# Broadcasting softmax factors through DRAM in an LSH attention kernel with a convolutional gate

## The chip, the cores and the metric

The kernel runs on one core of a Trainium2 chip. The metric is the time of one execution on the device in microseconds; the times given are medians of several runs. One further execution was profiled, and all rows of a profile come from that one.

## The reference

Attention with a hash mask runs over 4 batches, 8 heads, 768 positions and a head size of 64; a query sees only the keys whose 6 sign bits of a projection agree with its own. A gated feed-forward net (512 to 1024 to 512) follows, with a convolution of three taps along the sequence in the gate.

```python
mask = q_bucket[:, :, :, None] == k_bucket[:, :, None, :]
scores = scale * np.matmul(q, k.transpose(0, 1, 3, 2))
scores = np.where(mask, scores, -1000000000.0)
scores = scores - np.max(scores, axis=-1, keepdims=True)
attn = np.exp(scores)
attn = attn / (np.sum(attn, axis=-1, keepdims=True) + 1e-09)
x = np.matmul(attn, v)          # heads side by side: B, S, 512
h = np.maximum(x @ w_in, 0.0)
conv_out = sum(conv_w[k] * hp[:, k:k + S, :] for k in range(3))   # hp: h padded by one row
out = (h * (1.0 / (1.0 + np.exp(-conv_out)))) @ w_out
```

The weights of the feed-forward net come as 64-bit floats. The kernel splits them, as it splits x, q and k, into a high and a low part, so that matmuls on the fast 32-bit format keep their precision.

## The kernel before

**Pairs, groups, units.** Two heads form a *pair*; there are 16 (4 batches of 4). A *unit* is a tile of 128 queries of one head against all 768 keys, so a pair has 12 units. Four units (two heads, two query tiles, 256 queries) form a *group*, three groups to a pair. All units stand in one list, and one loop over `i` emits the instructions in a fixed order by hand; each engine executes its own instructions in that order. Iteration `i` emits, in this order: the score matmuls of unit `i` (`products`, L257), its maximum on VectorE (L270 and L274), the reciprocals of a group that has ended two units before (`reciprocals`, L291 and L292), the transposes of unit `i-3` (L297) and their copy to SBUF on ScalarE (L304), and the exponential of unit `i` on ScalarE (L277), which also sums the rows into one column of `sums`.

**The burst.** Once in four iterations, `AVS` gives a number of steps other than zero. Then the matmuls of probabilities and values of the group that was complete an iteration earlier go out in one burst: `values` gives its steps. The first step, `spread` (L319), multiplies a broadcast column of `inv` (a 128x64 weight whose 64 columns are all the reciprocals of one query tile and head) with the identity, four times. This puts the reciprocal of each query, repeated over the 64 rows of a head, into the second half of the PSUM tile `av`. Six `chunk` steps (L325) fill the first half. `factors` (L330, ScalarE, emitted at the start of the next iteration) copies the second half to the SBUF tile `rs`; `out` (L333, VectorE, in the next burst) multiplies the first half by it, and `parts` (L336 and L337, GpSimd) splits the result into the high and low part of x.

**Late pairs.** Pairs from number 7 on (`LATE`) normalise the probabilities themselves on GpSimd (L285) ahead of the transposes and use none of `reciprocals`, `spread`, `factors` and `rs`. The code that the change touches therefore runs for 7 pairs, 21 groups, in the first 230 us.

**What else is emitted around the burst.** In each burst some steps of decoding the feed-forward weights go out (`background`): integer operations on VectorE (L91 to L101), then a cast on ScalarE (L110) and two operations on GpSimd (L111 and L112). A weight block is loaded by a DMA on ScalarE's queue (`fetch`, L132). Beside them the next pair is prepared. The transposed q and k of a pair lie in `R`, which has one buffer. `split` forms the high part of a head on GpSimd (`hi`, L171), sends copies of it to the operand tiles by DMAs on SP's queue (L174), then forms the low part in `R` itself (L176) and sends that (L178). `hash` multiplies `R` with the projection (L186, TensorE, three iterations into the pair before the one that it is for). The seventh iteration of a pair ends the second `split`, and SP is then given the load of values (L165) and the next load of `R` (L158), which has to wait until the copies out of `R` have landed.

**The ending of a batch.** When all pairs of a batch and three pairs more are done, the feed-forward net of that batch runs (`ffn`; L368, L398 are its matmuls). The last group before it is handed to the net as `fill`, which emits that group's `values` steps at once within the net's first step. Of the pairs that use the reciprocals, this concerns one group.

Of the kernel before, what the change touches and what calls it, by code (L numbers as in the profile page):

```python
# [7 lines left out]
F32 = mybir.dt.float32  # L8
# [6 lines left out]
B, H, S, D = 4, 8, 768, 64  # L15
NB = 6
DM, DFF = 512, 1024
P = 128
NP = H // 2
NCK = S // P  # L20
HS = S // 2
QB = 256
# [7 lines left out]
LAG, EB = 3, 5  # L30
DEFER = 3
FLAG = 3
LATE = NP + DEFER
AVS = (1 + NCK, 0, 0, 0)
PREP = 1
PREP_N = 6
W0 = 7
# [5 lines left out]
def lsh_attention_conv_ffn(ctx, tc, qk, v, hw, w_in, conv_w, w_out, consts, ident_in, out):  # L43
    nc = tc.nc
    PSUM = bass.MemoryType.PSUM
    cp = ctx.enter_context(tc.tile_pool(name="const", bufs=1))
    wp = ctx.enter_context(tc.tile_pool(name="work", bufs=1))
    ps = ctx.enter_context(tc.tile_pool(name="ps", bufs=2, space=PSUM))

    turns = {}  # L50

    def ring(pool, bufs, shape, dtype, tag, name):

        k = turns[tag] = (turns.get(tag, -1) + 1) % bufs
        return pool.tile(shape, dtype, tag=f"{tag}{k}", name=name, bufs=1)
# [88 lines left out]
    class Pair:  # L144
        def __init__(self, b, p):
            self.b, self.p, self.nm = b, p, f"{b}_{p}"
            self.late = b * NP + p >= LATE
            self.inv = None

        def load(self):  # L150
            nm = self.nm
# [93 lines left out]
    class Unit:  # L245
# [14 lines left out]
        def maximum(self, prev):  # L260

            self.st = ring(wp, 8, [P, 4], F32, "st", f"st{self.nm}")
            pr = self.pair
            if self.tq == 0 and self.h == 0 and not pr.late:
                pr.sums = sums4[self.qb % 3]
            self.sums = None if pr.late else pr.sums
            self.sum = self.st[:, 2:3] if pr.late else pr.sums[:, 2 * self.tq + self.h, 0:1]
            e = wp.tile([P, 776], F32, tag="e", name=f"e{self.nm}", bufs=EB)
            self.e = e[:, :S]
            nc.vector.tensor_scalar(self.e.rearrange("p (a b) -> p a b", a=2), self.sp[:, :, :HS],  # L270
                                    MASKED, None, ALU.max, ALU.max, accum_out=self.st[:, 0:1])
            if prev and prev.pair.late:
                prev.total()
            nc.vector.tensor_scalar(self.st[:, 1:2], self.st[:, 0:1], -SCALE, None, ALU.mult)  # L274
# [12 lines left out]
        def reciprocals(self):  # L287
# [3 lines left out]
            nc.vector.tensor_reduce(pr.inv, self.sums, mybir.AxisListType.X, ALU.add)  # L291
            nc.vector.reciprocal(pr.inv, pr.inv)  # L292

        def transposes(self):
            self.tp = ring(ps, 3, [P, 2, 512], F32, "S", f"t{self.nm}")
            for c in range(NCK):
                nc.tensor.transpose(self.tp[:, c // 3, c % 3 * P:(c % 3 + 1) * P],  # L297
                                    self.e[:, c * P:(c + 1) * P], ident)
# [5 lines left out]
            nc.scalar.copy(pr.at[self.h][:, :, :, self.tq * P:(self.tq + 1) * P],  # L304
                           self.tp[:, :, :3 * P].rearrange("p j (c q) -> p j c q", c=3))

    def values(pr, qb, ats, inv):

        if qb == 0:
            pr.x = [ring(wp, NP + DEFER, [P, S], F32R, f"x{k}", f"x{k}{pr.nm}")  # L310
# [1 line left out]
        vt, (xh, xl) = pr.v, pr.x  # L312
        av = ring(ps, 2, [P, 512], F32, "M", f"v{pr.nm}_{qb}")

        def spread():

            for t in range(QB // P):
                for h in range(2):
                    nc.tensor.matmul(av[h * D:(h + 1) * D, QB + t * P:QB + (t + 1) * P],  # L319
                                     inv[:, 2 * t + h:2 * t + h + 1].to_broadcast([P, D]), ident,  # L320
                                     start=True, stop=True, tile_position=(0, h * D))

        def chunk(c):
            for h in range(2):
                nc.tensor.matmul(av[h * D:(h + 1) * D, :QB], vt[:, c, h, :],  # L325
                                 ats[h][:, c // 3, c % 3, :],
                                 start=(c == 0), stop=(c == NCK - 1), tile_position=(0, h * D))

        def factors():
            nc.scalar.copy(rs, av[:, QB:2 * QB])  # L330

        def out():
            nc.vector.tensor_tensor(rs, av[:, :QB], rs, ALU.mult)  # L333
# [12 lines left out]
        chunks = [lambda c=c: chunk(c) for c in range(NCK)]  # L346
        if pr.late:
            return chunks, (out_high, out_low, lambda: None)
        rs = ring(wp, 2, [P, QB], F32, "rs", f"rs{pr.nm}_{qb}")
        return [spread, *chunks], (factors, out, parts)  # L350


    g2, prep = [None], [iter(()), iter(())]
# [93 lines left out]
    first = pairs[0].prepare_now()  # L447
    next(first)
    pairs[1].load()
    av, outs, lows, early = [], [], [], None  # L450
    n = len(units)
    ffn_after = {min((b + 1) * NP - 1 + DEFER, B * NP - 1): b for b in range(B)}
    for i in range(n + LAG):
# [20 lines left out]
            prev.total()  # L474
        two = units[i - 2] if 2 <= i <= n + 1 else None
        if two and not two.pair.late and two.tq == QB // P - 1 and two.h == 1:
            two.reciprocals()
        if w and w is not early:
            w.transposes()
            w.to_sbuf()  # L480
# [1 line left out]
            u.exponential()  # L482
        if prev and prev.pair.late:
            prev.normalise()
        if i in (0, 2):
            next(first, None)
        parts = []
# [7 lines left out]
        prepare(0)  # L495
        if ending:
            prepare(0)
        for _ in range(1 + NCK if ending else AVS[(i - LAG) % 4]):
            if av:
                steps, last = av[0]  # L500
                steps.pop(0)()
                if not steps:
                    outs.append(last)
                    av.pop(0)
# [13 lines left out]
        fetch(i % 2 if i < 8 else burst)  # L518
        if w and w.tq == QB // P - 1 and w.h == 1:
            if not ending:  # L520
                av.append(values(w.pair, w.qb, w.pair.at, w.pair.inv))
            else:
                def fill():
                    steps, last = values(w.pair, w.qb, w.pair.at, w.pair.inv)
                    for step in [*steps, *last]:
                        step()

                bi = ffn_after[wi]
                early = units[i + 1 - LAG] if i + 1 - LAG < n else None

                def transposes_ahead():
                    if early:
                        early.transposes()
                        early.to_sbuf()
                        turns["S"] -= 1

                ffn(bi, [pairs[bi * NP + c].x for c in range(NCC)], fill, transposes_ahead)
# [43 lines left out]
```

## Time and profile before

| what | us |
|---|---|
| median of 3 runs (740.05 to 745.73) | 740.08 |
| the profiled execution | 739.48 |
| its span | 737.5 |
| TensorE matmul busy | 710.9 |
| VectorE busy | 487.3 |
| ScalarE busy | 498.5 |
| GpSimd busy | 331.9 |

In the profile's lines PE is TensorE's matmuls and PEld its weight loads, DVE is VectorE, ACT ScalarE, POOL GpSimd, SP the engine that only issues DMAs. A name with a q (SPq, ACTq) is the engine's queue, where the issue of a DMA counts. `L297` is line 297 of the kernel before. `t<-ident,e` reads: tile t is written from tiles ident and e; numbers in tile names are left out. What stands in brackets or behind a bar as "idle before" is the time for which the engine stood still ahead of the instruction, and what released it. TensorE's granted clock is 0.997 over the span. The chain of waits goes back from the last instruction, at each step to what released it. A matmul on 32-bit floats appears as two records, so four `spread` matmuls give eight.

### The profile page before, as it was taken

To read this page: it belongs to the slowest core of one execution; us is meant where nothing else is said; L and a number is where in the kernel's file an instruction comes from. 1 tells how busy PE (TensorE), PEld (TensorE's weight loads), DVE (VectorE), ACT (ScalarE), POOL (GpSimd) and SP (SyncE) were. 2 spreads that over 40 slices of the span, in tenths; PEclk is the share of its full clock that TensorE was granted. 3 is DMA by queue.
4 is the path that set the end of the run, shared out by engine and by line. 5 is a ranking of instruction groups with operands and counts; after the bars stand their busy time and mean duration, and the time that the engine had idled before them with its cause. 6 is when DMAs were issued, how large, how long until landed. Compare 5 with 4: busy or idle time off the path is not lost.

```text
span 737.5 us, 13543 instructions
## 1 busy us (share of the span) xinstructions
PE 710.9 (96%) x4720; PEld 589.0 (80%) x4720; DVE 487.3 (66%) x1211; ACT 498.5 (68%) x937; POOL 331.9 (45%) x334
## 2 busy tenths in 40 slices
PE   6998999899899999999999999999999999999997
PEld 3787777678778988777877998778778899878996
DVE  7977878788775755666665666466666566555663
ACT  5788578678684554877877554778778655585554
POOL 4265456357463522475673532355755232241321
PEclk9999999999999999999999999999999999999999
DMA  4867666663552310237545130324463001100011
GB/s 143 222 187 202 165 186 166 165 166 89 147 146 52 86 44 36 72 77 189 139 105 149 34 94 3 108 60 113 117 180 95 1 0 44 44 1 1 0 44 43
DMA packets 30355, 72.17 MB, mean 98 GB/s; under 512 B 5936, under 2 KB 7504, under 8 KB 30288
## 3 DMA queue, kind: packets, MB, share of 16 engines
q1 hardware_dynamic: 27696, 62.88, 32.0%
q10 hardware_dynamic: 2592, 8.44, 3.3%
q8 instruction: 37, 0.61, 0.3%
q14 instruction: 30, 0.25, 0.1%
HBM read 27.40 MB, written 6.29 MB: 46 GB/s over the span
## 4 chain that ended last, share of the span: by engine, by line
PE 69%; DMA 11%; POOL 7%; issue 5%; DVE 4%; SPq 3%; ACT 1%; POOLq 0%; DVEq 0%; ACTq 0%
PE h L368 19%; PE o L398 18%; PE v L325 11%; PE s L257 10%; PE t L297 9%; DMA R<-in_qk 6%; DMA k<-R 4%; POOL R L176 2%; SPq L174 2%; DVE e L270 1%; DMA K<-hi 1%; PE hash L186 1%; POOL hi L171 1%; ACT e L277 1%; SPq L178 1%
## 5 line engine op out<-in xcount | busy, mean ns | idle before, releaser
L270 DVE TENSOR_SCALAR_CACHE_REDUCE e<-s 128x768 f32<-128x768 f32 x192 | 183.2, 954 | 81.2 <-PE s L257 70.6
L277 ACT ACTIVATE e<-e,st 128x768 f32<-128x768 f32 x192 | 181.3, 944 | 10.3 <-DVE st L284 5.0
L304 ACT COPY at<-t 128x768 f32<-128x768 f32 x192 | 152.3, 794 | 47.0 <-PE t L297 47.0
L297 PE MATMUL t<-ident,e 128*128 128x128 f32 x1152 | 160.0, 275 | 3.6 <-POOL e L285 1.5
L377 DVE SCALAR_TENSOR_TENSOR ht<-ht,cw 128x384 f32<-128x384 f32 (+1 forms) x128 | 114.7, 896 | 71.2 <-ACT ht L375 69.0
L387 POOL TENSOR_TENSOR g<-ht,g 128x384 fp32r<-128x384 f32 x64 | 71.5, 1117 | 179.5 <-ACT g L386 141.8
L297 PEld LDWEIGHTS t<-ident,e 128*128 128x128 f32 x1152 | 130.6, 141 | 22.3 <-POOL e L285 7.4
L285 POOL TENSOR_SCALAR e<-e,st 128x768 f32<-128x768 f32 x108 | 98.3, 911 | 103.1 <-DVE st L284 51.4
L398 PE MATMUL o<-wo,g 128*128 128x512 f32 x576 | 142.4, 394 | 0.0
L368 PE MATMUL h<-xh,wi 128*128 128x386 f32 x512 | 141.9, 340 | 0.0
L325 PE MATMUL v<-at,v 128*64 128x256 f32 x1152 | 135.6, 385 | 0.0
L398 PEld LDWEIGHTS o<-wo,g 128*128 128x128 f32 x576 | 107.4, 188 | 20.3
L257 PE MATMUL s<-K,Q 128*128 128x384 f32 x384 | 116.7, 385 | 1.9 <-ACT e L277 1.0
L325 PEld LDWEIGHTS v<-at,v 128*64 128x64 f32 x1152 | 81.2, 138 | 42.4 <-issue 8.6
L257 PE MATMUL s<-k,q 96*128 96x384 f32 x384 | 100.2, 342 | 2.1 <-ACT q L237 1.9
L368 PEld LDWEIGHTS h<-xh,wi 128*128 128x128 f32 x512 | 94.1, 188 | 4.8 <-issue 1.8
L380 ACT ACTIVATE ht<-ht 128x384 f32<-128x384 f32 x64 | 33.6, 526 | 91.4 <-DVE ht L377 91.4
L368 PE MATMUL h<-xl,wi 128*128 128x386 f32 x256 | 86.7, 339 | 0.0
L257 PEld LDWEIGHTS s<-K,Q 128*128 128x128 f32 x384 | 59.0, 192 | 23.2 <-issue 16.6
L257 PEld LDWEIGHTS s<-k,q 96*128 96x128 f32 x384 | 70.7, 191 | 3.5 <-ACT q L237 3.0
L381 DVE TENSOR_TENSOR ht<-ht 128x384 f32<-128x384 f32 x64 | 40.2, 629 | 33.4 <-ACT ht L380 33.4
L176 POOL TENSOR_TENSOR R<-R,hi 128x768 fp32r<-128x768 f32 x30 | 56.6, 1886 | 0.2
(75 smaller groups left out, 586.0 us busy)
## 6 DMA issues: line engine op xcount, KB each, us to landing
R<-in_qk SPq DMA_DIRECT2D x15, 768.0 KB
K<-hi SPq DMA_DIRECT2D x60, 192.0 KB
v<-in_v SPq DMA_DIRECT2D x16, 384.0 KB
out<-osb SPq DMA_DIRECT2D x24, 256.0 KB
Q<-hi SPq DMA_DIRECT2D x30, 192.0 KB
q<-hi SPq DMA_DIRECT2D x30, 192.0 KB
Q<-R SPq DMA_DIRECT2D x30, 192.0 KB
k<-R SPq DMA_DIRECT2D x30, 192.0 KB
```

The source lines that it names most:

```text
L176: nc.gpsimd.tensor_tensor(lo, R, hi.bitcast(F32), ALU.subtract)
L257: nc.tensor.matmul(self.sp[:, half, :HS], A[:, h, qs], C[:, h, half * HS:(half + 1) * HS], start=(kk == 0), stop=(kk == 1))
L270: nc.vector.tensor_scalar(self.e.rearrange("p (a b) -> p a b", a=2), self.sp[:, :, :HS], MASKED, None, ALU.max, ALU.max, accum_out=self.st ...
L277: nc.scalar.activation(self.e, self.e, AF.Exp, bias=self.st[:, 1:2], scale=SCALE, accum_out=self.sum)
L285: nc.gpsimd.tensor_scalar(self.e, self.e, self.st[:, 3:4], 0.0, ALU.mult, ALU.add)
L297: nc.tensor.transpose(self.tp[:, c // 3, c % 3 * P:(c % 3 + 1) * P], self.e[:, c * P:(c + 1) * P], ident)
L304: nc.scalar.copy(pr.at[self.h][:, :, :, self.tq * P:(self.tq + 1) * P], self.tp[:, :, :3 * P].rearrange("p j (c q) -> p j c q", c=3))
L325: nc.tensor.matmul(av[h * D:(h + 1) * D, :QB], vt[:, c, h, :], ats[h][:, c // 3, c % 3, :], start=(c == 0), stop=(c == NCK - 1), tile_posi ...
L368: nc.tensor.matmul(hp[:, :HW], w, x[:, c0:c0 + HW], start=(n == 0), stop=(n == 3 * NCC - 1))
L377: nc.vector.scalar_tensor_tensor(t[:, a:z], ht[:, o + k - 1 + a:o + k - 1 + z], cw[:, f, k:k + 1], t[:, a:z], ALU.mult, ALU.add)
L387: nc.gpsimd.tensor_tensor(g[:, 1, :], t, g[:, 0, :].bitcast(F32), ALU.subtract)
L398: nc.tensor.matmul(op, l, r, start=(f == 0 and n == 0), stop=(f == NFC - 1 and n == 2))
```

## The change

The reciprocals no longer go through TensorE. When a group's reciprocals are done, `reciprocals` now makes three things: a tile `row` of 2 x 2 x 128 floats in DRAM (a ring of four), a tile `rs` of 128 x 256 in SBUF (a ring of two, as before), and a list of steps. `write` sends `inv`, 128 partitions of four floats, to `row` in the order head, query tile, query. `read` issues two DMAs, one for each head: 256 floats of `row` are read into each of 64 partitions of `rs`. All three DMAs stand on ScalarE's queue. The main loop keeps these lists in `spreads` and executes one step of each per iteration, right after the exponential: `write` in the iteration of `reciprocals` itself, nothing in the next, `read` in the one after that. That is the iteration of the burst.

`spread` and `factors` go, `values` takes `rs` instead of `inv`, and a burst has six steps instead of seven. The columns of `sums` are ordered by head first, so that `inv` has the order of `row`. At the end of a batch the steps that are left are executed ahead of the feed-forward net, for the one group that `fill` takes over.

```diff
-AVS = (1 + NCK, 0, 0, 0)
+AVS = (NCK, 0, 0, 0)
+    dp = ctx.enter_context(tc.tile_pool(name="dram", bufs=1, space=bass.MemoryType.DRAM))
-            self.sum = self.st[:, 2:3] if pr.late else pr.sums[:, 2 * self.tq + self.h, 0:1]
+            self.sum = self.st[:, 2:3] if pr.late else pr.sums[:, 2 * self.h + self.tq, 0:1]
             nc.vector.reciprocal(pr.inv, pr.inv)
+            inv = pr.inv
+            row = ring(dp, 4, [2, QB // P, P], F32, "row", f"row{self.nm}")
+            rs = pr.rs = ring(wp, 2, [P, QB], F32, "rs", f"rs{self.nm}")
+
+            def write():
+                nc.scalar.dma_start(row.rearrange("h t q -> q (h t)"), inv)
+
+            def read():
+                for h in range(2):
+                    nc.scalar.dma_start(rs[h * D:(h + 1) * D],
+                                        row[h].rearrange("t q -> (t q)").unsqueeze(0).to_broadcast([D, QB]))
+
+            return [write, None, read]
-        def spread():
-
-            for t in range(QB // P):
-                for h in range(2):
-                    nc.tensor.matmul(av[h * D:(h + 1) * D, QB + t * P:QB + (t + 1) * P],
-                                     inv[:, 2 * t + h:2 * t + h + 1].to_broadcast([P, D]), ident,
-                                     start=True, stop=True, tile_position=(0, h * D))
-        def factors():
-            nc.scalar.copy(rs, av[:, QB:2 * QB])
-        rs = ring(wp, 2, [P, QB], F32, "rs", f"rs{pr.nm}_{qb}")
-        return [spread, *chunks], (factors, out, parts)
+        return chunks, (lambda: None, out, parts)
-            two.reciprocals()
+            spreads.append(two.reciprocals())
             u.exponential()
         if prev and prev.pair.late:
             prev.normalise()
+        for steps in spreads:
+            if steps:
+                step = steps.pop(0)
+                if step:
+                    step()
-        for _ in range(1 + NCK if ending else AVS[(i - LAG) % 4]):
+        for _ in range(NCK if ending else AVS[(i - LAG) % 4]):
-                av.append(values(w.pair, w.qb, w.pair.at, w.pair.inv))
+                av.append(values(w.pair, w.qb, w.pair.at, w.pair.rs))
             else:
+                for steps in spreads:
+                    while steps:
+                        step = steps.pop(0)
+                        if step:
+                            step()
```

More of the change, by code (lines that the diff above doesn't have):

```diff
@@ L147, in __init__ @@
             self.late = b * NP + p >= LATE
-            self.inv = None
+            self.inv = self.rs = None
         def load(self):
@@ L305, in to_sbuf, with values @@
                            self.tp[:, :, :3 * P].rearrange("p j (c q) -> p j c q", c=3))
-    def values(pr, qb, ats, inv):
+    def values(pr, qb, ats, rs):
         if qb == 0:
@@ L449, in lsh_attention_conv_ffn @@
     pairs[1].load()
-    av, outs, lows, early = [], [], [], None
+    av, outs, lows, early, spreads = [], [], [], None, []
     n = len(units)
@@ L520, in lsh_attention_conv_ffn @@
             if not ending:
-                av.append(values(w.pair, w.qb, w.pair.at, w.pair.inv))
+                av.append(values(w.pair, w.qb, w.pair.at, w.pair.rs))
             else:
+                for steps in spreads:
[3 more added lines that the diff above has]
+                            step()
                 def fill():
-                    steps, last = values(w.pair, w.qb, w.pair.at, w.pair.inv)
+                    steps, last = values(w.pair, w.qb, w.pair.at, w.pair.rs)
                     for step in [*steps, *last]:
```

## The prediction

> **What bounds the kernel now.** I read the page first, then the costs of the two operations that go, then the weight-load row of one burst, the waits of TensorE, and last the chain of waits through the first 230 us, where the changed code runs.
>
> ```profile
> span 737.5 us, 13543 instructions
> PE 710.9 (96%) x4720; PEld 589.0 (80%) x4720; DVE 487.3 (66%) x1211; ACT 498.5 (68%) x937; POOL 331.9 (45%) x334
> PE 69%; DMA 11%; POOL 7%; issue 5%; DVE 4%; SPq 3%; ACT 1%; POOLq 0%; DVEq 0%; ACTq 0%
> ```
>
> TensorE looks full, so removing matmuls looks like pure gain. But 18% of the chain that ended last is DMA and POOL, and that share has a place. The groups of instructions by line and form give what is removed; columns are count, then busy us and mean ns, then the idle time before them.
>
> ```profile
> L319 PE MATMUL v<-ident,inv 128*64 128x128 f32 x168 | 13.8, 285 | 0.0
> L330 ACT COPY rs<-v 128x256 f32<-128x256 f32 x21 | 7.8, 371 | 18.2 <-PE v L325 15.6 <-PE t L297 1.3 <-DMA rawi<-in_w_in 1.2
> ```
>
> The 168 records are 21 groups of 8. What one group holds TensorE for is read better from the weight loads of one burst in the timeline (start, duration, operation):
>
> ```profile
> 62.39 0.42 PEld L319 LDWEIGHTS v<-ident,inv 128*64 128x64 f32 x8 [0.17 <-issue]
> 62.77 2.41 PEld L325 LDWEIGHTS v<-at,v 128*64 128x64 f32 x24
> 65.57 0.30 PEld L257 LDWEIGHTS s<-K,Q 128*128 128x128 f32 x2 [0.38 <-issue]
> ```
>
> From the first broadcast weight to the first weight of the values, 62.77 - 62.39 = 0.38 us. The 0.17 us ahead of it I leave where it is, since the change of tile shape stays and the values come next. So 21 x 0.38 = 8.0 us of TensorE go at most, less than the 13.8 us of the busy column, whose ends overlap.
>
> Does TensorE have to wait for something else in that stage? The hash matmuls of the next pair of heads, one burst of eight per pair, answer that (timeline, idle time in brackets; then the same wait summed over 13 to 230 us as us, times, longest):
>
> ```profile
> 73.51 0.85 PE L186 MATMUL hash<-R,hw_sb 128*32 128x384 f32 x8 [2.18 <-DMA R<-in_qk]
> 103.10 0.85 PE L186 MATMUL hash<-R,hw_sb 128*32 128x384 f32 x8 [0.49 <-DMA R<-in_qk]
> 133.70 0.85 PE L186 MATMUL hash<-R,hw_sb 128*32 128x384 f32 x8 [1.82 <-DMA R<-in_qk]
> 161.97 0.85 PE L186 MATMUL hash<-R,hw_sb 128*32 128x384 f32 x8 [0.28 <-DMA R<-in_qk]
> 192.02 0.85 PE L186 MATMUL hash<-R,hw_sb 128*32 128x384 f32 x8 [1.87 <-DMA R<-in_qk]
> 220.17 0.85 PE L186 MATMUL hash<-R,hw_sb 128*32 128x384 f32 x8 [1.48 <-DMA R<-in_qk]
> PE hash L186 <- DMA R<-in_qk: 8.3, 7, 2.2
> ```
>
> From 73 us on, TensorE runs out of work at every pair because the load of R is late. The chain shows why; first its way into this state, then one full loop, then the end of it.
>
> ```profile
> 34.50 0.59 PE v L319 x8
> ...
> 44.20 0.59 PE v L319 x8
> ...
> 53.06 0.59 PE v L319 x8
> ...
> 62.73 0.60 SPq L178
> ...
> 63.38 3.98 DMA k<-R
> ...
> 67.37 6.00 DMA R<-in_qk
> ```
>
> ```profile
> 162.82 0.59 PE v L319 x8
> ...
> 173.68 2.89 issue
> ...
> 176.61 1.30 POOL upo L111
> ...
> 180.46 1.78 POOL R L176
> ...
> 183.54 3.93 DMA k<-R
> ...
> 187.53 4.36 DMA R<-in_qk
> ```
>
> ```profile
> 223.33 0.59 PE v L319 x8
> ```
>
> R has one buffer. It can be loaded again only when GpSimd has formed the low part in place (L176) and the copies of it (k<-R) have landed. GpSimd gets to L176 late because L111 ahead of it waits for ScalarE's cast of a weight block (L110), which belongs to the second burst of a pair. So a loop runs: R landed, hash, first burst of the pair, one group of four units, second burst, cast, L111, L176, copies, load of R. Only the first burst's matmuls are in it; the other two bursts of a pair run beside the copies and the load.
>
> **The change part by part.** Removed from TensorE: 0.38 us in each of 21 bursts. On the chain lie the bursts at 34.50, 44.20 and 53.06, one in each of the five loops between the six hash rows, and the one in the FFN's first step at 223.33: 9 x 0.38 = 3.4 us gained. The first burst (before 34.50) and two per loop, 12 x 0.38 = 4.6 us, only lengthen the wait for R.
>
> Removed from ScalarE: the copy `factors`, 0.37 us per group. Its row has 15.6 us of idle time before it that ended with TensorE, so ScalarE was waiting there anyway: nothing gained. The sums' new index and the six-step bursts cost nothing: no instruction is added by them, and no engine's order changes but for the eight records that go. The second half of the PSUM tile falls free, but the tile keeps its size and ring: nothing.
>
> Added, 21 times: one write of `inv` to DRAM and two reads of `row` into `rs`, all three on ScalarE's queue. ScalarE's order around a second burst, and the DMA rows to price it:
>
> ```profile
> 51.27 0.95 ACT L277 ACTIVATE e<-e,st 128x768 f32<-128x768 f32 x1
> ...
> 52.88 0.95 ACT L277 ACTIVATE e<-e,st 128x768 f32<-128x768 f32 x1
> ...
> 54.49 0.96 ACT L277 ACTIVATE e<-e,st 128x768 f32<-128x768 f32 x1
> ...
> 56.21 0.62 ACT L110 CAST wi<-upi 128x512 fp32r<-128x512 f32 x1 [0.68 <-DVE lowi L101]
> 57.67 0.33 ACTq L132 DMA_DIRECT2D rawi<-in_w_in  x1
> ```
>
> ```profile
> 61.40 1.23 SPq L174 DMA_DIRECT2D K<-hi  x2
> ```
>
> ```profile
> 136.47 1.95 DMA K<-hi
> ```
>
> ```profile
> q10 hardware_dynamic: 2592, 8.44, 3.3%
> ```
>
> ```profile
> 211.90:215.90 4.00, 4.00 (x35) 3.00 (x30) 2.97 (x5) 2.61 (x6) 1.53 (x2) 1.00 1.02 261
> 215.90:220.10 4.20, 2.68 (x19) 2.09 (x17) 3.25 (x15) 3.99 (x8) 3.53 (x5) 1.00 0.63 205
> ```
>
> The write follows the exponential two units after a group's last, here the one at 51.27; the wait it brings is for the reciprocals, which VectorE forms right behind the maximum that this exponential needs too, so they are done while it runs. Its issue (0.33 us for a load from this queue, 0.61 us for a 64-partition copy) hides behind the 0.95 us as well. Without that cover it would cost 0.3 to 0.6 us of ScalarE.
>
> The reads follow two exponentials later, at 54.49, and wait for the write to land. 54.49 - 51.27 = 3.2 us are there; a copy between SBUF tiles landed 1.95 us after its issue, so I take no hold here. No row shows a write of single floats to DRAM, so this is bounded below. Queued behind the two reads on ScalarE are the cast L110, the weight loads of L132 and the next unit's copy of transposes; GpSimd waits for the cast, and so does the loop. Two issues at 0.61 us end 1.2 us after the exponential starts, 0.3 us past its end (1.2 - 0.95). In the quoted burst the cast had 0.68 us of idle time ahead of it, in others none: between 0 and 1.2 us, I take 0.3 us per loop.
>
> The landed factors are wanted by VectorE's product (L333) a burst later, 62.39 - 53.06 = 9.3 us after. Behind it in its queue stand the decoding steps of a weight block, the next maximum and so the cast; cover of about 7 us after a landing like the 1.95 us one makes this wait nothing.
>
> What the transfers do to others: the last burst of a pair puts its reads beside the critical k<-R, when the 16 engines are full (1.02 in the first window; the column before the last is the DMA share). Two halves of 64 rows of 1 KB are 131 KB: at 261 GB/s 0.5 us if they are only added, 0 if they fit into gaps; I take 0.4 us. The write of the following group falls into the load of R. `inv` has four floats per partition that go to places 512 bytes apart, so I count 512 packets, 32 per engine. Queue q10 took 3.3% of 16 engines' 737.5 us for 2592 packets, 0.15 us each, mostly of 4 KB. That gives 32 x 0.15 = 4.8 us per engine if a packet of one float costs as much, and nearly 0 if the cost goes by bytes. With a share of 0.63 in the second window, 0.37 x 4.2 = 1.6 us per engine are free; I take 0.3 us of delay, near the lower end, because those gaps cover the first 1.6 us. Per loop 0.3 + 0.4 + 0.3 = 1.0 us, over the six loads of R 6.0 us. That the transfers themselves bring a gain is excluded: none of the old ones goes away.
>
> At the last group of the stage the read is flushed one unit after the write, not two, so ScalarE may hold there for most of a landing, under 2 us; TensorE itself waits for R until 220.17 at that place, so I put it at nothing. SP's and POOL's queues issue nothing new and nothing is moved past them, other than through what they wait for.
>
> Sum on the profiled execution, 739.48 us (span 737.5, 2.0 outside it; 0.6 below the median of 740.08): 739.5 - 3.4 + 6.0 = 742.1 us.
>
> **The rivals.** *All matmuls pay.* If the loop of R were not the limit, all 8.0 us would go: 731.5 us. For it: two of the six waits are only 0.28 and 0.49 us. Against: they alternate with waits of 1.8 us and more, and each shorter group of TensorE makes R later relative to it. If the loop limits but the transfers are free, 739.5 - 3.4 = 736.1; I count this into the forecast's own range.
>
> *The write lands late and holds ScalarE: slower.* The read sits in front of the cast at the second burst of each pair. With 512 packets at 0.15 us, landing takes 1.95 + 4.8 = 6.75 us, 3.55 us more than the 3.2 available, six times: 21 us, 763 us. It decides against the kernel by 1% from a hold of 0.9 us per loop, (747.5 - 742.1) / 6, a landing of 4.1 us or 67 ns per packet. For it: nothing in the trace writes single floats, so nothing shows that they are cheap. Against: the packets carry 2 KB in all. The Trainium skill, DMA: Bandwidth & Descriptors, section Rules for kernel authors, states that an access with a strided last dimension becomes one descriptor per element and advises against it; no run here shows it yet, and by that rule this rival's packet count holds.
>
> *The change doesn't do what it says*: if something still kept the two-step order waiting, such as the product L333 arriving before the factors, TensorE would idle at bursts. 9.3 us of cover speak against; I give it no chance of its own.
>
> **How the numbers follow.** About 1%, 7.4 us, is what can be told from no change. Forecast 0.58, from 736 to 747. All matmuls pay 0.12, 731 to 735: a little over half of it, 0.07, is faster by over 1%. Late landing 0.30, 747.5 to 763, nearly all slower. So faster 0.07, same 0.63, slower 0.30. For 8 in 10 the range takes the forecast's own, the upper half of the first rival and half of the late landing: 734 to 754. The forecast's own range is 736 to 747.
>
> **What would show it.** Right: no records of L319's kind; weight loads of the values 0.38 us earlier in a burst; hash waits for R longer than before, near 2 us in every pair; k<-R or the load of R a few tenths longer; the last hash (220.17) about 3 us later at most. Wrong: hash waits that vanish (then all 8 us pay), or the cast L110 held on ScalarE by a write in DRAM, seen as idle time ended by a DMA ahead of it, and L111 later in step. If the period from hash to hash, about 29.3 us ((220.17 - 73.51) / 5), shrinks to three bare groups of TensorE, the loop was not the limit.

## The result and the profile after

The kernel after takes 837.85 us (median of 4 runs, 830.33 to 841.61), the kernel before beside it 740.07 us: ratio 1.129, 95% interval 1.124 to 1.134. I had predicted 742.1 us and a range up to 754. Both the side and the size are wrong: 98 us are lost where 2 were expected.

The page of the kernel after, with the granted clock by slices and the row of ScalarE's DMA queue (packets, MB, share of 16 engines):

```profile
span 839.8 us, 13315 instructions
PE 739.0 (88%) x4552; PEld 609.0 (73%) x4552; DVE 488.4 (58%) x1211; ACT 493.6 (59%) x916; POOL 330.5 (39%) x334
PEclk8898899779888888999999999999999999999999
q10 hardware_dynamic: 17040, 11.24, 5.9%
```

What was to go is gone: 4720 - 4552 = 168 matmuls, 937 - 916 = 21 copies. The other engines are as busy as before and the span is 102 us longer, so the time is waiting. The clock shows where: it is at 0.7 to 0.9 in the first sixteen slices, some 336 us with the stage of the changed code, and then does not fall below 0.9. Queue q10 has 17040 - 2592 = 14448 packets more, 688 for each of 21 groups: 512 for the write as counted, 128 for the rows that are read, and 48 more, 16 for each of the three transfers (the kernel with the write alone, further down, has 528 for each group).

The hash matmuls of TensorE in the timeline, the marks of the loop of R (L187 here is L186 of before):

```profile
98.92 1.03 PE L187 MATMUL hash<-R,hw_sb 128*32 128x384 f32 x8
...
231.83 1.51 PE L187 MATMUL hash<-R,hw_sb 128*32 128x384 f32 x8 [6.08 <-DMA R<-in_qk]
274.26 1.51 PE L187 MATMUL hash<-R,hw_sb 128*32 128x384 f32 x8 [5.50 <-DMA R<-in_qk]
317.46 0.99 PE L187 MATMUL hash<-R,hw_sb 128*32 128x384 f32 x8
```

The last of them comes at 317.46 instead of 220.17 us. So 97.3 of the 102 us are lost in this stage, and a pair takes (317.46 - 98.92) / 5 = 43.7 us instead of 29.3.

ScalarE and its queue in the timeline: the issue of a write (L300), of the two reads that wait for it (L304), and the cast behind them (L111 here, L110 before).

```profile
62.22 0.38 ACTq L300 DMA_DIRECT2D row<-inv  x1
...
74.20 1.10 ACTq L304 DMA_DIRECT2D rs<-row  x2
75.39 0.62 ACT L111 CAST wi<-upi 128x512 fp32r<-128x512 f32 x1 [6.93 <-DMA q<-bits]
...
241.21 0.37 ACTq L300 DMA_DIRECT2D row<-inv  x1
...
251.85 1.36 ACTq L304 DMA_DIRECT2D rs<-row  x2
```

Between issue and reads lie 12.0 and 10.6 us, in the 21 groups 7.8 to 12.9. I had 3.2 us there and a landing of 1.95. The cast stands behind the reads, as one rival had it; its bracket names a transfer of the bits (`q<-bits`), the last to land of those that were waited for there. The other transfers suffer too; rows of the chain of waits (start, duration):

```profile
82.22 9.01 DMA k<-R
91.28 6.46 DMA R<-in_qk
...
220.32 11.38 DMA R<-in_qk
...
264.62 9.51 DMA R<-in_qk
```

In the prediction's rows the same two took 3.93 to 3.98 and 4.36 to 6.00 us. And yet the DMA engines are idle most of that time. The window between a write's issue and its reads (columns: us, busy of PE, PEld, DVE, ACT, POOL, granted clock, DMA share, GB/s):

```profile
241.20:251.90 10.70, 7.54 (x58) 6.51 (x56) 7.68 (x20) 4.30 (x9) 2.79 (x3) 1.00 0.24 47
```

A share of 0.24 means that something else than the time of packets on the engines holds the write up. The write issued at 108.69 us shows it by itself. This row is ScalarE's queue between 109.5 and 110.1 us, with the packets of that write; between 110.1 and 117.0 us the queue has none, and yet the reads start only at 117.13.

```profile
q10 hardware_dynamic: 528, 0.00, 45.8%
```

The waits over the whole kernel (us, times, longest) show who pays in the end:

```profile
DVE e L271 <- PE s L258: 151.7, 81, 6.7
POOL upi L112 <- ACT wi L111: 82.3, 8, 19.7
PEld s L258 <- ACT at L319: 59.5, 21, 6.2
```

ScalarE's copies stand behind the held reads, the scores' weights wait for them (59.5 us), and VectorE waits for the scores. SP's queue waits as well: four of its waits, 11.1 us in all, end with the landing of a write, though nothing on SP reads `row`. The prediction has no such path, and why SP waits there no run tests. The same view for SP's queue (13 to 330 us):

```profile
SPq L179 <- DMA row<-inv: 5.9, 2, 4.1
SPq L196 <- DMA row<-inv: 5.2, 2, 3.7
```

### The profile page after: what moved, and what is told of

Same layout as the page of the kernel before. It is cut to its first block, busy times and chain, and to the rows that moved or that the text cites. A ratio compares the mean times of both kernels' runs of the same rounds, so it can differ in the third digit from the quotient of the medians.

```text
span 839.8 us, 13315 instructions
## 1 busy us (share of the span) xinstructions
PE 739.0 (88%) x4552; PEld 609.0 (73%) x4552; DVE 488.4 (58%) x1211; ACT 493.6 (59%) x916; POOL 330.5 (39%) x334
## 3 DMA queue, kind: packets, MB, share of 16 engines
q10 hardware_dynamic: 17040, 11.24, 5.9%
## 4 chain that ended last, share of the span: by engine, by line
PE 57%; DMA 18%; issue 10%; POOL 7%; DVE 3%; SPq 3%; ACT 1%; ACTq 0%; POOLq 0%; DVEq 0%
PE h L371 16%; PE o L401 16%; PE v L332 8%; PE s L258 8%; PE t L312 8%; DMA R<-in_qk 5%; DMA k<-R 4%; DMA Q<-hi 2%; POOL R L177 2%; DMA row<-inv 1%; DVE e L271 1%; SPq L196 1%; POOL hi L172 1%; SPq L175 1%; DMA Q<-R 1%
## 5 line engine op out<-in xcount | busy, mean ns | idle before, releaser
L312 PE MATMUL t<-ident,e 128*128 128x128 f32 x1152 | 173.3, 291 | 10.9 <-DVE e L271 9.0
L258 PE MATMUL s<-K,Q 128*128 128x384 f32 x384 | 124.2, 407 | 56.5 <-ACT at L319 44.9
L312 PEld LDWEIGHTS t<-ident,e 128*128 128x128 f32 x1152 | 143.3, 150 | 30.3 <-DVE e L271 11.0
L332 PE MATMUL v<-at,v 128*64 128x256 f32 x1152 | 143.5, 398 | 2.0 <-ACT at L319 2.0
L332 PEld LDWEIGHTS v<-at,v 128*64 128x64 f32 x1152 | 85.1, 143 | 54.9 <-issue 21.4
L258 PEld LDWEIGHTS s<-K,Q 128*128 128x128 f32 x384 | 63.2, 205 | 81.0 <-ACT at L319 59.5
L258 PE MATMUL s<-k,q 96*128 96x384 f32 x384 | 105.6, 358 | 2.3 <-ACT q L238 2.3
L258 PEld LDWEIGHTS s<-k,q 96*128 96x128 f32 x384 | 76.1, 205 | 3.2 <-ACT q L238 3.2
```

Of the source, the lines that this page charges most:

```text
L258: nc.tensor.matmul(self.sp[:, half, :HS], A[:, h, qs], C[:, h, half * HS:(half + 1) * HS], start=(kk == 0), stop=(kk == 1))
```

## The experiments

Ratios are to the kernel before on the same chip, with 95% intervals. Where none is given, the kernel ran once, and a few us are then not told from none: runs of the kernel before lie between 739.9 and 747.3 us on one chip. The diffs give the lines that carry an experiment, not all that follow from them.

### Do the matmuls pay, and does the hold matter?

Two theories stood at first. By the hold, the late landing of the write keeps ScalarE's queue waiting, with the copies and casts in it. By the packets, 512 small packets load the 16 DMA engines and delay what else is on them. Beside them stood the question of what the removal alone brings.

**No transfers at all.** `one` is a constant tile.

```diff
-            return [write, None, read]
+            return [None, None, None]
-            nc.vector.tensor_tensor(rs, av[:, :QB], rs, ALU.mult)
+            nc.vector.tensor_tensor(rs, av[:, :QB], one, ALU.mult)
```

> The changed kernel without its three DMAs per group; the product takes a constant in place of the factors, so the normalisation is left out. What is left is the gain of the removed matmuls. If the load of R limits the stage, as the prediction had it, 3.4 us are gained: about 736.5 us. If all 21 bursts pay, 8.0 us: about 732 us. By both theories of the slowdown (a held ScalarE, or traffic of small packets) it is gone here.

Measured: 744.78 us against 743.80, 1.002 (0.999 to 1.004). Without any transfer the 168 matmuls and 21 copies bring nothing; the 3.4 us expected did not come. The wait of the six hashes on the load of R, first without the matmuls, then before (window from 60 to 225 us):

```profile
PE hash L188 <- DMA R<-in_qk: 12.1, 6, 3.1
```

```profile
PE hash L186 <- DMA R<-in_qk: 8.1, 6, 2.2
```

The wait grew by 4.0 us; the prediction had 4.6 us of lengthening. The two ends of the stage without the matmuls:

```profile
72.40 1.51 PE L188 MATMUL hash<-R,hw_sb 128*32 128x384 f32 x8 [2.71 <-DMA R<-in_qk]
...
219.62 1.51 PE L188 MATMUL hash<-R,hw_sb 128*32 128x384 f32 x8 [3.07 <-DMA R<-in_qk]
```

From first to last 147.2 us, before 146.7: the loop of R did not become shorter by the 0.38 us per pair that the prediction put in it.

**Reads that wait for nothing**: they take the row of two groups before, so ScalarE isn't held by a fresh write.

```diff
+            rows.append(row)
+            old = rows[-3] if len(rows) > 2 else ident_in[0:4].rearrange("(h t) q -> h t q", h=2)
-                                        row[h].rearrange("t q -> (t q)").unsqueeze(0).to_broadcast([D, QB]))
+                                        old[h].rearrange("t q -> (t q)").unsqueeze(0).to_broadcast([D, QB]))
```

> All three DMAs of every group stay, in their places, but the reads take the row written two groups earlier (an input for the first two groups), so that ScalarE does not wait for the write just issued. The factors are another group's, so the result is not the attention. Theory A, the reads hold ScalarE until the write has landed: the hold goes and the time falls to 736 to 745 us. Theory B, the 512 small packets slow the other transfers and so the load of R: the packets are all there, the time stays above 800 us.

Measured: 881.7 us, 1.187 (1.180 to 1.194), slower still than the change. So the hold alone is not the cause. The time went to the load of R. A hash of it in the timeline, and the sum of its waits (window 20 to 360 us):

```profile
163.28 1.51 PE L188 MATMUL hash<-R,hw_sb 128*32 128x384 f32 x8 [13.39 <-DMA R<-in_qk]
```

```profile
PE hash L188 <- DMA R<-in_qk: 51.5, 6, 13.4
```

That load took 19.08 us, the 11.65 us landing of a write is as in the change; both are rows of its chain:

```profile
51.19 11.65 DMA row<-inv
...
144.07 19.08 DMA R<-in_qk
```

**Reads two iterations later.**

```diff
-            return [write, None, read]
+            if pr.b * NP + pr.p == LATE - 1 and self.qb == 1:
+                return [write, None, read]
+            return [write, None, None, None, read]
```

> The reads stand two iterations later, so four iterations lie between write and read instead of two, about 9 us in place of 3.2 (one group keeps the old place). In the changed kernel the read is issued 8.2 to 12 us after the write. Theory A: most of the hold goes, 0 to 3 us are left per group, 740 to 775 us. Theory B: above 800 us.

Measured: 862.15 us, 1.157 (1.153 to 1.161): slower than the change too. Room for the landing does not help. Why both unheld kernels are slower than the held one is not settled.

**Write alone.** `values` multiplies by a constant.

```diff
-            return [write, None, read]
+            return [write, None, None]
-            nc.vector.tensor_tensor(rs, av[:, :QB], rs, ALU.mult)
+            nc.vector.tensor_tensor(rs, av[:, :QB], one, ALU.mult)
```

> The changed kernel with the write of 512 floats in each group, without the reads; the product takes a constant, so the normalisation is left out. Nothing waits for the write. Theory B (the write's packets hold up every other transfer for about 10 us): the load of R and the copies out of it are late, hash waits of 5 us and more, 800 us or more. If the reads were what disturbs: near the kernel without transfers, 742 to 748 us.

Measured: 851.72 us against 743.91. The whole loss is there although nothing in the kernel reads what is written. Rows of its chain, a write, then copies out of R and loads of R that later writes lie beside:

```profile
24.09 10.12 DMA row<-inv
...
87.43 9.41 DMA k<-R
96.90 12.06 DMA R<-in_qk
```

The window of the next load of R:

```profile
143.28:153.55 10.27, 5.24 (x20) 4.64 (x20) 2.57 (x7) 3.45 (x6) 0.00 (x0) 0.67 0.38 111
```

A load that took 4 to 6 us before takes 10 with the engines busy for 0.38 of the time, and TensorE idles for half of it.

**Reads alone**, from an input.

```diff
-            row = ring(dp, 4, [2, QB // P, P], F32, "row", f"row{self.nm}")
+            row = ident_in[0:4].rearrange("(h t) q -> h t q", h=2)
-            return [write, None, read]
+            return [None, None, read]
```

> The two reads of each group stay, from an input in place of the scratch, and there is no write; the factors are not those of the softmax. Theory B: the reads are cheap, 131 KB per group, 742 to 752 us. If the reads carried the loss: above 780 us.

Measured: 750.67 us, 1.008 (1.003 to 1.012), against 1.002 without any transfer: 0.006 x 744 = 4.5 us for the 42 reads, by the two intervals between about 1 and 8. The prediction's terms for them were (0.3 + 0.4) x 6 = 4.2.

### What is it about the write?

**Half of the packets.** Half of the floats are written, 256 packets.

```diff
-                nc.scalar.dma_start(row.rearrange("h t q -> q (h t)"), inv)
+                nc.scalar.dma_start(row.rearrange("h t q -> q (h t)"), inv[:, :QB // P])
```

> Only head 0's reciprocals are written, 256 floats, and read for both heads, so that the factors of head 1 are wrong. From 512 packets landing in 9.3 to 11.9 us and 128 packets of 16 bytes in 3.4 to 4.4 us, a line of about 0.22 us for each of the packets that an engine gets, over 1.9 us: 16 packets per engine land in about 5.4 us, and the time falls between 760 and 838 us, near 785. If the landing does not depend on the count: 830 us or more.

Measured: 842.47 us, no less than the change. I had expected far less, a miss that was worth more than a hit. Its write and reads in the timeline, and the landing of another write in its chain:

```profile
50.79 0.38 ACTq L300 DMA_DIRECT2D row<-inv  x1
...
63.64 1.11 ACTq L304 DMA_DIRECT2D rs<-row  x2
```

```profile
83.32 11.02 DMA row<-inv
```

12.9 us between write and reads, and 11.0 for a landing, with half of the packets: their number isn't the price. What stayed the same is that 16 floats lie in each 64 bytes.

**Rows of 16 bytes**, a partition's four floats side by side, 128 packets.

```diff
-            row = ring(dp, 4, [2, QB // P, P], F32, "row", f"row{self.nm}")
+            row = ring(dp, 4, [P, 2 * QB // P], F32, "row", f"row{self.nm}")
-                nc.scalar.dma_start(row.rearrange("h t q -> q (h t)"), inv)
+                nc.scalar.dma_start(row, inv)
```

> The write stores the four floats of a partition side by side: 128 packets of 16 bytes in place of 512 of 4. The reads take as many bytes as before, contiguous, in the wrong order, so the factors are wrong. Theory A with a landing that grows with the packets: about 2 us + (11 - 2)/4 = 4.3 us, a hold of 1 us, 740 to 760 us. Theory A with a landing that any write to DRAM has: unchanged, near 838 us. Theory B: a quarter of the packets, about 765 us.

Measured: 759.87 us, 1.022 (1.018 to 1.026). Most of the loss is gone, at a quarter of the packets. Since half of them changed nothing, a third theory, the sharing (theory C): single floats from different partitions go to the same few bytes of DRAM (16 of them to each 64 bytes, since `row` has the queries side by side), and such writes wait for each other. Four kernels with the write alone vary how many floats share 64 bytes. All are made from the kernel with the write alone:

```diff
# each float in its own 64 bytes, 512 packets
+            row = ring(dp, 4, [2 * QB // P, P, 16], F32, "row", f"row{self.nm}")
+                nc.scalar.dma_start(row[:, :, 0].rearrange("c q -> q c"), inv)
# each float in its own 512 bytes, 512 packets
+            row = ring(dp, 4, [2 * QB // P, P, 128], F32, "row", f"row{self.nm}")
# floats of a partition 8 bytes apart, two partitions to 64 bytes, 512 packets
+            row = ring(dp, 4, [P, 2 * QB // P, 2], F32, "row", f"row{self.nm}")
+                nc.scalar.dma_start(row[:, :, 0], inv)
# rows of 16 bytes, four to 64 bytes, 128 packets
+            row = ring(dp, 4, [P, 2 * QB // P], F32, "row", f"row{self.nm}")
+                nc.scalar.dma_start(row, inv)
```

> As the kernel with the write alone (852 us): no reads, a constant in place of the factors. The same 512 packets of 4 bytes, but each float goes to its own 64 bytes of DRAM instead of next to the floats of the neighbouring partitions. Theory C, small writes into the same few lines of DRAM wait for each other: the loss is gone or falls below a third, 745 to 780 us. Theory D, each small packet costs, wherever it goes: unchanged, 840 to 860 us.

> The same with 512 bytes of DRAM for each float, 256 KB of scratch in place of 2 KB. Theory C: 745 to 780 us, and if the unit that writes contend for is larger than 64 bytes, clearly faster than with 64 bytes. Theory D: 840 to 860 us.

> The write alone, 512 packets of 4 bytes, with the four floats of a partition 8 bytes apart in 32 bytes of their own, so that 64 bytes of DRAM take 8 packets from 2 partitions where the write alone had 16 packets from 16. Theory C with writes of different DMA engines as what collides: fast, 745 to 780 us. Theory C with any writes to the same line: between, 780 to 830 us. Theory D: 840 to 860 us.

> The write alone as 128 packets of 16 bytes, four partitions to 64 bytes; no reads. With the reads this layout took 760 us. Theory C, 4 packets to a line where the write alone had 16: about a quarter of the loss or less, 745 to 770 us. Theory D with the loss in proportion to the packets: about (852 - 745)/4 more than without transfers, 772 us.

| write alone | packets | packets to 64 bytes | us |
|---|---|---|---|
| kernel before on that chip | | | 742.5 |
| as in the change (another chip, before 743.9) | 512 | 16 | 851.7 |
| floats 8 bytes apart | 512 | 8 | 773.5 |
| rows of 16 bytes | 128 | 4 | 745.1 |
| each in its own 64 bytes | 512 | 1 | 740.4 |
| each in its own 512 bytes | 512 | 1 | 746.4 |

With 512 packets the loss follows the number that share 64 bytes: 108 us for 16, 31 for 8 and, for one, -2 and 4, which single runs can't tell from nothing. The rows of 16 bytes, four to 64 bytes, cost 3, but they are fewer as well. None of these kernels reads its rows back. Half of the packets with the same sharing taking as long would fit writes to one place going one after the other and places side by side; that is argued, not shown. Of the theories, the sharing holds. How large the piece of memory is within which packets wait for each other stays open: the layouts also differ in the memory that one write covers, from 2 to 256 KB. Rows of the chains, first with each float in its own 64 bytes, then with floats 8 bytes apart:

```profile
98.40 4.53 DMA R<-in_qk
...
159.01 2.87 DMA row<-inv
```

```profile
110.66 7.90 DMA R<-in_qk
...
211.34 8.87 DMA R<-in_qk
```

In these rows a write without sharing lands in 2.87 us and the load of R is back at 4.5 us; with eight packets to 64 bytes the loads of the chain take 7.1 to 8.9 us, one of them 4.3. What the sharing does inside the memory or the engines no run shows.

### A version without the cause

**Turned first.** One matmul turns `inv` into four rows of 128 floats ahead of the write, which then goes out as four runs of 512 bytes.

```diff
+        def turn(self):
+            nc.tensor.matmul(self.tp[:4, 0, HS:], self.pair.inv, ident, start=True, stop=True)
+                nc.scalar.copy(w.turned, w.tp[:4, 0, HS:])
-                nc.scalar.dma_start(row.rearrange("h t q -> q (h t)"), inv)
+                nc.scalar.dma_start(row.rearrange("h t q -> (h t) q"), turned)
-            return [write, None, read]
+            return [None, write, None, read]
```

> The change without colliding writes, with the right result: one matmul (in place of four) turns the 128x4 reciprocals into 4 rows of 128 in a free part of the PSUM tile of the transposes, ScalarE copies them to SBUF, and the write to DRAM is 4 rows of 512 bytes; the reads as in the change, one iteration later. Theory C: the loss of the change goes, and what is left is near the kernel with the reads alone, 740 to 752 us. If DMAs behind each other (a write, a wait, two reads) were the loss, whatever the layout: above 780 us.

Measured: 765.62 us, 1.031 (1.027 to 1.036), above the 740 to 752 expected. 76 of the 98 us are gone, 22 remain. Its waits in the window 20 to 250 us show ScalarE held still:

```profile
PEld s L258 <- ACT at L324: 13.3, 11, 3.3
DVE rs L342 <- DMA rs<-row: 8.4, 6, 3.4
```

**Turned, and read one iteration later.**

```diff
-            return [None, write, None, read]
+            return [None, write, None, None, read]
```

> The version with turned rows (766 us), its reads one more iteration later, right result. If what is left of the loss there (22 us) is ScalarE held by the reads until the write has landed: most of it goes, 745 to 755 us. If the reads and the write cost it by their traffic: unchanged, 762 to 768 us.

Measured: 766.52 us, 1.031 (1.026 to 1.035). The hold went from ScalarE to VectorE, the same rows in the window 20 to 260 us:

```profile
DVE rs L342 <- DMA rs<-row: 23.3, 18, 4.5
PEld s L258 <- ACT at L324: 5.0, 5, 1.4
```

In both places tried for the reads one of the queues pays. None of the kernels that compute the whole reference is faster than the kernel before. How much of the 22 us is this hold, and how much the added matmul and copy, is open.

### Why the removed matmuls bring nothing

**Half the load of R** in the kernel before (the lower 64 partitions alone), to see whether the loop of R limits.

```diff
-                nc.sync.dma_start(self.R.bitcast(F32), src)
+                nc.sync.dma_start(self.R[:64].bitcast(F32), src[:64])
```

> The kernel before, but from the second pair on only q is loaded into R (64 of its 128 rows) and k is left as an old one was, so the result is another one; every operation and every other transfer stays. If the late load of R is what holds TensorE at the hash, the waits shrink by about 2 us each: 728 to 737 us. If something else takes its place: 740 or more.

Measured: 734.87 us, 0.990 (0.987 to 0.993). The loop does limit. First and last hash:

```profile
73.70 0.85 PE L188 MATMUL hash<-R,hw_sb 128*32 128x384 f32 x8 [1.99 <-DMA R<-in_qk]
...
217.47 0.85 PE L188 MATMUL hash<-R,hw_sb 128*32 128x384 f32 x8 [1.12 <-DMA R<-in_qk]
```

143.8 us instead of 146.7. But the load is not shorter: in the chain the half takes 4.4 to 5.8 us, the whole in the kernel before 4.1 to 6.0. It starts sooner. The lower half of R is free when the copy `Q<-R` has landed, and SP issues that copy 0.5 to 0.8 us ahead of `k<-R`, which stands in this place in the kernel before. That half of the bytes also leaves other transfers more room is not separated from this. Rows of the last loop:

```profile
208.76 3.98 DMA Q<-R
...
212.81 4.53 DMA R<-in_qk
```

**The same without the matmuls** (and without transfers).

```diff
# the kernel without transfers, and
-                nc.sync.dma_start(self.R.bitcast(F32), src)
+                nc.sync.dma_start(self.R[:64].bitcast(F32), src[:64])
```

> The same half load in the changed kernel without its transfers, which had no gain over the kernel before with the whole load. If the load of R swallowed the gain, up to 8.0 us of it appear now: 4 to 8 us less than the half load with the matmuls. If the removed matmuls are worth nothing for another reason: the same time as with them.

Measured: 740.24 us, 0.996 (0.994 to 0.998): 0.6% slower than with the matmuls (5.4 us by the medians), where 4 to 8 us of gain were expected. An earlier load did not set the gain free.

**R in two tiles**, one for each head, so that half of it can load earlier, in the kernel before.

```diff
-            self.R = ring(wp, 1, [P, 2, S], F32R, "R", f"R{nm}")
+            self.R[h] = ring(wp, 1, [P, S], F32R, f"R{h}_", f"R{self.nm}_{h}")
...
+        if u and k == PREP + PREP_N - 1 and pi + 2 < len(pairs):
+            pairs[pi + 2].load_half(0)
```

> The kernel before, matmuls and all, with R as two tiles, one for each head, and the load of the first head given to SP one iteration earlier, ahead of the last step of the split. Half of the load then lies off the loop of R. If that loop limits the first 220 us, the waits of the hash for R (8.3 us in all) shrink by most of their length: 732 to 737 us where the kernel before has 741 to 744 on that chip. If TensorE limits it: no change.

Measured: 749.77 us, 1.009 (1.005 to 1.012), slower; the test says nothing on the loop, since it moves other transfers as well.

**The clock.** Without the matmuls TensorE waits longer at the hash, and its granted clock drops behind a long wait. In the next two kernels eight idle matmuls ahead of each hash fill the wait: once in the kernel without transfers, once in that with the half load too.

```diff
+        if i == 86 or (k == PREP + 2 and 24 <= i < 86):
+            for _ in range(8):
+                nc.tensor.matmul(free[0], ident, ident, start=True, stop=True)
```

> The changed kernel without its transfers (constant in place of the factors), with 8 matmuls of the identity by itself, whose result nobody reads, ahead of the hash of each pair where TensorE waits for R: about 1.1 us of work put into the wait. Without them that kernel was level with the kernel before (ratio 1.0017), with waits of 2.3 us and more followed by 3 to 6.5 us at half the granted clock. If those stretches are what the removed matmuls' gain went into, the idle time now stays under about 2 us, the clock stays up, and the kernel is 3 to 6 us faster than without the filling: ratio 0.993 to 0.998. If the clock is a bystander: up to 1 us slower than without, ratio 1.002 or above.

> Half of the load of R, no transfers, no broadcast matmuls, and the 8 idle matmuls ahead of each hash. With the half load, the kernel with the broadcast matmuls ran at a ratio of 0.9898 to the kernel before, the one without them at 0.9959, with a lower clock (0.987 against 0.996 in the mean of the runs). If the lower clock is the difference: ratio 0.988 to 0.991 here. If it is not: 0.994 or above.

Measured: 745.49 us, 1.002 (1.000 to 1.005), and 739.12 us, 0.994 (0.992 to 0.997). The clock is back (0.995 in both profiled executions, 0.985 and 0.988 without the filling), the time is not. So no gain from the clock is to be seen. The filling may cost time of its own, though: at three of these six hashes of the first kernel no wait is left ahead of the hash. First and last hash of the first of the two:

```profile
74.34 0.85 PE L188 MATMUL hash<-R,hw_sb 128*32 128x384 f32 x8 [1.05 <-DMA R<-in_qk]
...
222.19 0.85 PE L188 MATMUL hash<-R,hw_sb 128*32 128x384 f32 x8 [3.10 <-DMA R<-in_qk]
```

147.9 us. The loop of R keeps its pace whatever TensorE leaves out.

**What the traces point at** is SP's queue, which the prediction's loop doesn't have. Ahead of the copies of the low part it gives out the copies of the bits and of `hi`. The low part of a head on GpSimd and the issue of its first copy in the last loop, first in the kernel before, then in the kernel without transfers:

```profile
209.24 1.83 POOL L176 TENSOR_TENSOR R<-R,hi 128x768 fp32r<-128x768 f32 x1
...
211.10 0.71 SPq L178 DMA_DIRECT2D Q<-R  x1
```

```profile
207.16 1.83 POOL L178 TENSOR_TENSOR R<-R,hi 128x768 fp32r<-128x768 f32 x1
...
208.10 1.83 SPq L176 DMA_DIRECT2D K<-hi  x2
...
210.03 0.56 SPq L180 DMA_DIRECT2D Q<-R  x1
```

Before, SP issues the copy as the low part ends (211.07). Without the matmuls the low part ends at 208.99, and SP is still giving out copies of `hi`: the copy waits 1.0 us. Over the five loops between the six hashes this wait sums to 2.01 us in place of 0.65. That would be 1.36 of the 2.4 us that are missing between the 1.9 us expected (5 x 0.38) and the 0.5 us lost (147.2 against 146.7). It is read from one trace of each kernel, and no run tests it; the rest stays open.

## Why the prediction was wrong

**The step that failed** is the price of the write: "I take 0.3 us of delay, near the lower end", from a range of 0 to 4.8 us per engine that came from q10's 0.15 us per packet, and with it the landing of 1.95 us from a copy between SBUF tiles. Both ends counted packets or bytes. The packet count was right, 512, but the price depends on something that neither has in it, the number of packets that go to the same bytes: in the change the reads follow 7.8 to 12.9 us after the write's issue, and while writes were under way the load of R took 6 to 11 us. A pair lost far more than the 1.0 us of the sum: 43.7 - 29.3 = 14.4. The write's own term was 6 x 0.3 = 1.8 us; the kernel with the write alone takes 851.7 us, 107 more than the 744.8 of the kernel without transfers (on two chips). The kernel with 64 bytes for each float has no loss to be seen.

**The rival that lands late** had the right beginning and was given 0.30: 6.75 us of landing against 7.8 to 12.9. The nearness is luck, since the 6.75 came from a price for each packet, and half of the packets land no sooner. Its path, the hold of the cast on ScalarE, exists in the trace. But its price of 21 us was a fifth of what came, for it left out the other transfers; and with the hold removed the time rose to 881.7 us. The Trainium skill, DMA: Bandwidth & Descriptors, section Rules for kernel authors, makes a descriptor of each element of a strided access and advises against it: the trace agrees on the count, 512, and own bytes for each show that the count alone is harmless here (740.4 us). The same page of the Trainium skill, section Specifications, says that below 512 bytes the engine reads, modifies and writes. Floats in their own 64 bytes are below 512 as well and cost nothing to be seen, so this alone is not the price; whether it makes neighbours wait for each other no run shows.

**The gain** of 9 x 0.38 = 3.4 us failed too, unseen beside the loss: 1.002 (0.999 to 1.004) without transfers. Right in it: the 8 records of a burst went, the loop of R limits (an earlier load gives 1%), the waits for R grew by 4.0 us where 4.6 were put. Wrong: that each loop gets shorter by its first burst; the traces show SP's queue as a second limit beside it, which no run tests. The rival that all matmuls pay (731.5 us) falls with it.

**Held up:** the reads together, 4.2 us put and about 4.5 measured, with an uncertainty of nearly as much; that each of their two terms is right no run shows. **The size** of the sum was therefore off in two terms, of which the write's is nearly all.

**What would show it** named the cast held by a write in DRAM, which came, but no sign for a load of R that takes twice its time.

## What to carry to other kernels

Cost a small write to DRAM by where its packets land, and not alone by how many there are or what they carry: floats of different partitions put side by side cost some 5 us a write here (108 / 21), in 64 bytes of their own nothing to be seen, and turned to runs of 512 bytes first most of the loss went. Look at what else is under way while such a write lands; the transfers beside it pay, and moving the waiting reads does not help. Work taken from an engine that waits in every round for a transfer gave longer waits here: expect nothing until a run shows that the transfer came earlier, and count the queue that issues the transfers as a part of the loop.

## What the runs showed of the hardware

After a write of 2 KB in packets of 4 bytes, 16 to each 64 bytes of DRAM, the reads that wait for it start 7.8 to 12.9 us after its issue, with half of the packets 8.5 to 12.9, though one such write's packets had all gone 1.4 us after the issue (110.1 against 108.69). Copies and loads beside it take about twice their time at a DMA share of 0.24 to 0.38. The same packets in their own 64 bytes land in 2.87 us, with a load of R at 4.5 us.

The granted clock can drop to 0.50 behind a short wait of TensorE. Windows of the kernel before behind its hash at 73.51, ahead of which TensorE waited 2.18 us:

```profile
75.00:76.00 1.00, 1.00 (x8) 0.57 (x6) 0.96 (x3) 0.00 (x0) 1.00 (x2) 0.50 0.63 139
...
77.00:78.00 1.00, 1.00 (x6) 0.50 (x5) 0.97 (x2) 0.00 (x0) 1.00 (x2) 0.50 1.03 240
```

The clock is at half for about 3 us although TensorE is busy. A wait of about 2 us can be enough, but the length doesn't decide it alone. Behind the quoted waits of 1.48 to 1.87 us the clock stays full in the windows looked at, and so it does behind the 3.10 us at 222.19 in the kernel with the filled wait. Behind 2.71 us in the kernel without transfers it dropped. The Trainium skill, TensorE: Matmul & The Clock Gate, Part 1, speaks of a window of about 3.4 us that runs freely and of a throttle after an idle one: a free-running window fits that waits of like length end differently, while 2.18 us is less than the idle window that it names.
